# Routing two chunks at once in a convolution and mixture-of-experts kernel, and a written order for the tile loads

## The chip, the cores and the metric

The kernel runs on one core of one Trainium2 chip. The metric is the time of one execution in device microseconds (us). The core's engines are TensorE (PE; PEld is its weight load), VectorE (DVE), ScalarE (ACT), GpSimd (POOL) and SyncE (SP, which here only issues transfers). The 16 DMA engines carry what SP and POOL issue.

## The reference

A causal convolution of width 7, whose weights differ per position and head (softmax over the seven taps), gives x of 28672 rows by 192. Each row then goes to one of eight experts, the one with the highest logit, and the expert's two-layer network is scaled by the gate's probability:

```
w = softmax(weight_gen, axis=-1)                      # (8, 3584, 8, 7)
x[s, h, g] = sum_k w[s, h, k] * x_pad[s + k, h, g]     # 28672 x 192
logits = x @ w_gate;  e = argmax(logits);  gate = softmax(logits)[e]
y = gate * (relu(x @ w1[e]) @ w2[e])                   # w1 192x1024, w2 1024x192
```

## The kernel before

The rows are worked in 28 chunks of 1024 (128 partitions by J = 8 columns). For a chunk c, DVE makes the convolution (`taps`: seven multiplications and six additions of 1536 elements per partition, written as L386 and L410; the first five chunks get help from PE and POOL), ACT and DVE split the result into two f16 parts in the payload buffer `pl` (`high`, `low`, three buffers), PE transposes it (L506), and `finish(c)` routes it: 24 small matmuls for the logits (`logits`), a row of short DVE operations that find the expert (`route1`), nine narrow matmuls that count ranks (`ranks`), the gate factor (`gate`), the place of every row in its expert's queue (`places`), and `send(c)`, in which POOL scatters the chunk's eight columns of rows to the `queue` in DRAM by eight indirect transfers (helper line L589). At the end `choose(c)` runs `select` (seven short DVE operations, L603 to L618), which takes as many full tiles of 384 rows from the eight queues as the plan says. `make_plan` fixes that number before the run: it keeps up to HOLD = 6 tiles' worth of rows back, so that every tile taken is of one expert. Chunks 1 to 4 give tiles of 256 rows, chunks 5 to 26 two or three tiles of 384 (one for chunk 5), chunk 27 the rest: tiles of 384, 256 and 128 and padded short ones.

`experts()` works the tiles n = 0, 1, 2, ... in order. `fetch(n)` issues on SP: a load of the tile's first row number from `rows` (L809, waits for `select`), the transposed rows `xt` (L825, waits until the scatters of all chunks up to the tile's chunk have landed), the expert's weights `wt` (L827, 1.8 MB, three buffers, so it waits until PE has ended the second layer of tile n - 3) and `meta` (L830, the rows' gate factor and destination). PE makes the first layer (L890, five matmuls for each of eight groups), ACT the relu `hh` (L910), DVE the low part `hl` (L913), PE the second layer (L787), ACT the scaled output `o` (L791, six buffers), and POOL scatters `o` to the output (L589). The first-layer results stand in four PSUM buffers `ph`, the second-layer results in four `y` slots. For some tiles PE and ACT make the low part in place of DVE (L899, L903, L905).

DVE's order is written out by the program: a planner holds a clock of DVE (`clock[0]`) and of PE (`clock[1]`), takes the low parts when they are due, then routing steps, then the convolution, and adds a cost for each. The other engines' order comes from the scheduler of the framework, which goes by its own estimate and by priorities; routing steps stand at high priority. Each engine works its instructions in order.

Of the kernel before, what the change touches and what calls it, by code (L numbers as in the profile page):

```python
# [28 lines left out]
ROW = 392  # L29
# [3 lines left out]
J = 8  # L33
# [3 lines left out]
SUBS = 6  # L37
LATE_SUBS = 18
STEP = 0.2
# [80 lines left out]
def conv_moe_kernel(ctx: ExitStack, tc: tile.TileContext, x, wgen, w_gate, w1, w2, out):  # L120
# [42 lines left out]
    nc.vector.tensor_scalar(negi, identf, -1.0, None, op0=ALU.mult)  # L163
    revE = const.tile([P, J, E], F32, name="revE")
    nc.gpsimd.iota(revE, pattern=[[0, J], [-1, E]], base=E, channel_multiplier=0,
                   allow_small_or_imprecise_dtypes=True)
# [5 lines left out]
    nc.vector.tensor_scalar(room, base0[0:1, :], -1.0, float(TOP), op0=ALU.mult, op1=ALU.add)  # L172
    oh_t = []
    for i in range(2):
        t = const.tile([P, J + 1, E], F16, name=f"oh{i}")
        nc.gpsimd.memset(t, 0.0)
        oh_t.append(t)
    eg_t = []
    for i in range(2):
        t = const.tile([P, J, E + 1], F32, name=f"eg{i}")  # L180
        nc.gpsimd.memset(t[:, :, E:], 1e-9)
        eg_t.append(t)
# [270 lines left out]
    def scale(c):  # L453
# [57 lines left out]

    def logits(c):
        k = ch[c]
        k.pm = ps_m.tile([P, 512], F32, name="pm")
        k.lp = k.pm[:, 0:J * 2 * E].rearrange("p (j t e) -> p j t e", j=J, t=2)
        for j in range(J):
            for n in range(3):
                nc.tensor.matmul(k.lp[:, j], k.xg[:, 3 * j + n, :], gw[:, n], start=(n == 0), stop=(n == 2))  # L518
                clock[1] += GATE

    def route1(c):
        k = ch[c]
        k.lg = rt.tile([P, J, E], F32, name="lg")
        k.eg = eg_t[c % 2]
        nc.vector.tensor_reduce(k.lg, k.lp.rearrange("p j t e -> p j e t"), axis=AX.X, op=ALU.add)
        yield STEP
        lm = rt.tile([P, J], F32, name="lm")
        nc.vector.tensor_reduce(lm, k.lg, axis=AX.X, op=ALU.max)
        yield STEP
        nc.vector.tensor_tensor(k.lg, k.lg, lm.unsqueeze(2).to_broadcast([P, J, E]), op=ALU.subtract)  # L530
        nc.scalar.activation(k.eg[:, :, 0:E], k.lg, AF.Exp, scale=k.lsc)
        yield STEP
        pri = rt.tile([P, J, E], F32, name="pri")
        nc.vector.scalar_tensor_tensor(pri, k.lg, 0.0, revE, op0=ALU.is_ge, op1=ALU.mult)
        yield STEP
        pmx = rt.tile([P, J], F32, name="pmx")
        nc.vector.tensor_reduce(pmx, pri, axis=AX.X, op=ALU.max)
        yield STEP
        k.oh = oh_t[c % 2]
        nc.vector.tensor_tensor(k.oh[:, 0:J, :], pri, pmx.unsqueeze(2).to_broadcast([P, J, E]), op=ALU.is_equal)  # L540

    def ranks(c):
        k = ch[c]
        k.rp = k.pm[:, 256:256 + (J + 1) * E].rearrange("p (j e) -> p j e", j=J + 1)
        nc.tensor.matmul(k.rp, tri, k.oh, start=True, stop=False)
        for j in range(J):
            nc.tensor.matmul(k.rp[:, j + 1:, :], ones_h, k.oh[:, j:j + 1, :].to_broadcast([P, J - j, E]),
                             start=False, stop=(j == J - 1))
        clock[1] += 0.3

    def gate(c):
        k = ch[c]
        se = rt.tile([P, J], F32, name="se")
        nc.vector.tensor_reduce(se, k.eg, axis=AX.X, op=ALU.add)
        yield STEP
        nc.vector.tensor_tensor(se, se, k.rsx.to_broadcast([P, J]), op=ALU.mult)
        yield STEP
        nc.vector.reciprocal(k.pl.bitcast(F32)[:, :, D], se)
        yield STEP

    def places(c):
        k = ch[c]
        rk = rt.tile([P, J, E], F32, name="rk")
        bs = base[-1]
        nc.vector.tensor_tensor(rk, k.rp[:, 0:J, :], bs.unsqueeze(1).to_broadcast([P, J, E]), op=ALU.add)
        nb = rt.tile([P, E], F32, name="nb", bufs=3)
        nc.vector.tensor_tensor(nb, k.rp[:, J, :], bs, op=ALU.add)
        base.append(nb)
        yield STEP
        nc.vector.tensor_tensor(rk, rk, k.oh[:, 0:J, :], op=ALU.mult)  # L570
        yield STEP
        k.pos = rt.tile([P, J], I32, name="pos")
        with nc.allow_low_precision("queue positions are whole numbers below 2**24"):
            nc.vector.tensor_reduce(k.pos, rk, axis=AX.X, op=ALU.add)
        yield STEP

    def send(c):
        k = ch[c]
        for j in range(J):
            st = scatter(queue, k.pos[:, j:j + 1], k.pl[:, j, 0:ROW // 2], "q")  # L580
            tc.add_to_no_dep_group(f"s{c}", st.ins)
            writers[c].append(st.ins.name)
        sent[0] = c
# [84 lines left out]
    rest = []  # L668
    first_ = []
    sent = [0]  # L670
    writers = [[] for _ in range(NCH)]
# [122 lines left out]
    def fetch(n):  # L794
# [44 lines left out]
    def experts():  # L839
# [25 lines left out]
        while True:  # L865
# [13 lines left out]
            for t in range(groups):  # L879
# [253 lines left out]
```

## Time and profile before

| what | value |
|---|---|
| median of 3 runs | 1186.94 us (1186.53 to 1188.32) |
| the profiled execution | 1185.47 us |
| its span in the profile | 1183.8 us |
| PE busy | 1123.8 us, 95% of the span |
| DVE busy | 1034.9 us, 87% |
| POOL busy | 696.3 us, 59% |
| ACT busy | 647.1 us, 55% |

The span runs from the first to the last instruction in the profile; 1.7 us of the profiled execution lie around it. Busy shares are averages over stages: the first fifth of the span is the start, with the weights' preparation and the first chunks; then convolution and experts run side by side until the last chunk is routed near 1012 us; from there on only tiles are left.

### The profile page before, as it was taken

What the parts mean: (1) busy time and instruction counts of PE and PEld (TensorE: products, weight loads), DVE (VectorE), ACT (ScalarE), POOL (GpSimd) and SP (SyncE); (2) the same over time, 40 slices, a digit from 0 to 9 for tenths busy, and PEclk for the clock granted to TensorE, in tenths of its full rate; (3) what the DMA queues carried; (4) which work ended last, traced back from release to release, by engine and by line L of the source; (5) the groups of instructions that cost most, each with busy time, mean ns of one, the idle gap of its engine ahead of it and who ended that gap; (6) DMA issues with size and microseconds to landing.
All of it is one profiled execution on the core that took longest, in us unless ns stands there. A gap on an engine that the chain in (4) does not pass through costs nothing. (4 is left out here: it accounts for less than half of the span.)

```text
span 1183.8 us, 29289 instructions
## 1 busy us (share of the span) xinstructions
PE 1123.8 (95%) x11327; PEld 913.1 (77%) x11327; DVE 1034.9 (87%) x1771; ACT 647.1 (55%) x1348; POOL 696.3 (59%) x633
## 2 busy tenths in 40 slices
PE   5689799999999999999999999999999999999996
PEld 3455489998778878787788888787777777778996
DVE  7999999999999999999999999999999997833231
ACT  3555477777556555545554555656465556443342
POOL 7998647766654654664566566447555675721222
PEclk9999899999999999999999999999999999999999
DMA  9989899999889787888898788777687666799993
GB/s 280 378 299 335 248 335 308 307 307 307 254 219 279 239 257 229 258 240 232 221 290 237 209 276 260 234 209 236 235 242 245 196 151 223 235 330 353 351 344 136
DMA packets 182847, 311.44 MB, mean 263 GB/s; under 512 B 131243, under 2 KB 154785, under 8 KB 167470
## 3 DMA queue, kind: packets, MB, share of 16 engines
q1 hardware_dynamic: 160702, 264.17, 73.3%
q0 software_dynamic: 22000, 45.33, 12.0%
q8 instruction: 91, 1.49, 0.5%
q14 instruction: 54, 0.44, 0.1%
HBM read 226.97 MB, written 60.45 MB: 243 GB/s over the span
## 5 line engine op out<-in xcount | busy, mean ns | idle before, releaser
L890 PE MATMUL ph<-xt,wt 128*128 128x384 f16 (+6 forms) x3680 | 571.2, 296 | 9.5 <-DVE hl L913 5.5
L787 PE MATMUL yo<-wt,hh 128*128 128x192 f16 (+1 forms) x3648 | 489.8, 246 | 2.9 <-ACT o L791 2.9
L589 POOL DMA_INDIRECT out_dram<-o,meta x228 | 281.1, 1233 | 323.5 <-ACT o L791 254.5
L787 PE MATMUL yo<-wt,hl 128*128 128x192 f16 (+1 forms) x1824 | 438.3, 246 | 0.0
L890 PEld LDWEIGHTS <-wt 128*128 128x128 f16 x3680 | 317.7, 98 | 124.3 <-issue 6.4
L910 ACT ACTIVATE hh<-ph 128x384 f16<-128x384 f32 (+2 forms) x485 | 238.5, 495 | 292.9 <-PE ph L890 272.1
L913 DVE SCALAR_TENSOR_TENSOR hl<-ph,hh 128x384 f16<-128x384 f32 (+2 forms) x485 | 260.4, 552 | 110.7 <-ACT hh L910 110.2
L787 PEld LDWEIGHTS <-hh 128*128 128x128 f16 (+1 forms) x3648 | 330.2, 98 | 32.9 <-issue 3.7
L589 POOL DMA_INDIRECT queue<-pl,pos x224 | 289.7, 1293 | 98.6 <-issue 72.9
L386 DVE TENSOR_TENSOR tv<-x_sb,wp 128x1536 f32<-128x1536 f32 (+1 forms) x173 | 286.2, 1656 | 1.7 <-PE ph L395 1.4
L410 DVE TENSOR_TENSOR acc<-acc,tv 128x1536 f32<-128x1536 f32 x138 | 239.6, 1736 | 0.0
L787 PEld LDWEIGHTS <-hl 128*128 128x128 f16 (+1 forms) x1824 | 178.7, 98 | 18.5 <-ACT hl L905 0.2
L791 ACT ACTIVATE o<-yo,fac 128x192 f32<-128x192 f32 (+1 forms) x228 | 90.5, 418 | 89.5 <-PE yo L787 85.1
L508 ACT ACTIVATE xg<-ph 128x1024 f16<-128x1024 f16 x84 | 81.6, 1022 | 38.2 <-PE ph L506 38.0
L395 PE MATMUL ph<-tv,identf 128*128 128x384 f32 x210 | 82.6, 539 | 17.8 <-DVE tv L386 17.1
L395 PEld LDWEIGHTS ph<-tv,identf 128*128 128x128 f32 x210 | 41.4, 209 | 45.2 <-DVE tv L386 19.0
L899 ACT ACTIVATE hh<-ph 128x512 f16<-128x512 f32 (+1 forms) x88 | 48.9, 562 | 22.1 <-PE ph L890 16.0
L447 ACT ACTIVATE junk<-x_sb 128x768 bf16<-128x768 f32 (+2 forms) x56 | 48.0, 857 | 16.1 <-DVE ssq L456 6.0
L905 ACT ACTIVATE hl<-ph 128x512 f16<-128x512 f32 (+1 forms) x88 | 47.7, 559 | 10.6 <-PE ph L903 10.2
L506 PE MATMUL ph<-idh,pl 128*128 128x128 f16 x672 | 52.3, 219 | 0.4 <-DVE pl L500 0.3
L486 ACT ACTIVATE pl<-acc 128x768 f16<-128x768 f32 (+1 forms) x51 | 39.0, 805 | 15.3 <-DVE acc L410 9.2
L506 PEld LDWEIGHTS <-pl 128*128 128x128 f16 x672 | 42.7, 98 | 5.9 <-ACT pl L491 2.6
(133 smaller groups left out, 768.9 us busy)
## 6 DMA issues: line engine op xcount, KB each, us to landing
wt<-wq SPq DMA_DIRECT2D x92, 1796.0 KB
x_sb<-in_x_dram SPq DMA_DIRECT2D x27, 1344.0 KB
w_sb<-in_weight_gen_dram SPq DMA_DIRECT2D x28, 224.0 KB
wq<-ws SPq DMA_DIRECT2D x8, 772.0 KB
f<-in_moe_w_dram SPq DMA_DIRECT2D x8, 768.0 KB
f<-in_moe_w_dram SPq DMA_DIRECT2D x8, 512.0 KB
wq<-ws SPq DMA_DIRECT2D x8, 512.0 KB
wq<-ws SPq DMA_DIRECT2D x32, 128.0 KB
```

The costliest lines, as they stand in the source:

```text
L386: eng.tensor_tensor(out, xs, ws, op=ALU.mult)
L395: nc.tensor.matmul(ap[:, 0:m], identf, tf[:, 2 * i * D:2 * i * D + m], start=(n == 0), stop=(n == KW - 1))
L410: eng.tensor_tensor(ac, ac, t, op=ALU.add)
L506: nc.tensor.transpose(pt[:, m, :], p16[:, j, n * P:(n + 1) * P], idh)
L508: nc.scalar.activation(k.xg[:, i:i + 8, :], pt, AF.Copy)
L589: st = nc.gpsimd.indirect_dma_start(out=dst, out_offset=bass.IndirectOffsetOnAxis(ap=idx, axis=0), in_=src, in_offset=None, **kw)
L787: nc.tensor.matmul(y, hx[:, f, sl], w2v[:, f, t, :], start=(f == 0 and k == 0), stop=(f == NF - 1 and k == 2))
L791: nc.scalar.activation(o[0:m, :], y, AF.Copy, scale=fac[0:m, s:s + 1])
L890: nc.tensor.matmul(ph[:, g], wt[:, wc + f * P:wc + (f + 1) * P], xt[:, xc, 0:T], start=(k == 0 and g == 0), stop=(k == 4), skip_group_chec ...
L899: nc.scalar.activation(hv, ph, AF.Relu, scale=SHRINK)
L910: nc.scalar.activation(hv, ph, AF.Relu)
L913: nc.vector.scalar_tensor_tensor(lv, ph, 0.0, hv, op0=ALU.max, op1=ALU.subtract)
```

## The change

Four pairs of chunks, (6, 7), (8, 9), (10, 11) and (12, 13), are routed together. The first chunk of a pair ends after its logits matmuls, which go to the first half of a PSUM tile that both share; the second chunk's routing then works on both at once, with operands twice as wide, sends the rows of both (16 indirect transfers in a row) and chooses the tiles of both in one `select`. `make_plan` gives the first of a pair no tile and the second those of both (5, 6, 5 and 5 tiles); the number and sizes of all tiles stay as they were. New buffers: a third one-hot tile `oh` and exponent tile `eg` of double width, each with a memset on POOL at the start; `revE` is a row that is broadcast. The reciprocal in `gate` and the exponential on ACT stay one for each chunk.

On SP, an order is written down: for tiles of chunks 18 to 26 the weights are issued before the transposed rows, which follow them; for tiles of chunks 5 to 15 the rows follow `meta` of the tile before. The last line of the diff writes a condition in another way, with the same tiles on either side of it.

```diff
+PAIRED = (6, 8, 10, 12)
+LATE_FROM = 18
@@ t_main
-        return [T_MAIN]
+        return [] if c in PAIRED else [T_MAIN]
...
@@ scale
-        k.rsx = rt.tile([P, 1], F32, name="rsx", bufs=4)
+        if c - 1 in PAIRED:
+            k.rsx = ch[c - 1].rsx2[:, 1:2]
+        else:
+            k.rsx2 = rt.tile([P, 2], F32, name="rsx", bufs=4)
+            k.rsx = k.rsx2[:, 0:1]
@@ logits
+        at = 0
+        if c - 1 in PAIRED:
+            k.pm, at = ch[c - 1].pm, J
+        else:
+            k.pm = ps_m.tile([P, 512], F32, name="pm")
+        k.n = at + J
+        k.lp = k.pm[:, 0:k.n * 2 * E].rearrange("p (j t e) -> p j t e", j=k.n, t=2)
...
+    def members(c):
+        return [ch[c - 1], ch[c]] if ch[c].n > J else [ch[c]]
@@ route1
+        n = k.n
+        sh = [P, n, E]
...
+        nc.vector.tensor_tensor(lg, lg, lm.unsqueeze(2).to_broadcast(sh), op=ALU.subtract)
+        for i, m in enumerate(members(c)):
+            nc.scalar.activation(k.eg[:, i * J:i * J + J, 0:E], lg[:, i * J:i * J + J], AF.Exp, scale=m.lsc)
...
@@ ranks
+        k.rp = k.pm[:, 256:256 + (n + 1) * E].rearrange("p (j e) -> p j e", j=n + 1)
         nc.tensor.matmul(k.rp, tri, k.oh, start=True, stop=False)
+        for j in range(n):
+            nc.tensor.matmul(k.rp[:, j + 1:, :], ones_h, k.oh[:, j:j + 1, :].to_broadcast([P, n - j, E]),
+                             start=False, stop=(j == n - 1))
@@ gate
+        for i, m in enumerate(ms):
+            nc.vector.reciprocal(m.pl.bitcast(F32)[:, :, D], se[:, i * J:i * J + J])
+            yield STEP
...
@@ send
+        for i, k in enumerate(members(c)):
+            for j in range(J):
+                st = scatter(queue, ch[c].pos[:, i * J + j:i * J + j + 1], k.pl[:, j, 0:ROW // 2], "q")
...
@@ finish
         logits(c)
+        if c in PAIRED:
+            return
         yield from route1(c)
@@ fetch
-        rows_of(nc.sync.dma_start_transpose(xt[:, :, 0:T], q16[ds(r, T), 0:2 * D]))
         wt = pw.tile([P, WROW], F16, name="wt")
-        nc.sync.dma_start(wt, wq[ds(e * P, P), :])
+        behind = LATE_FROM <= c < NCH - 1
+        if behind:
+            before_[:] = [nc.sync.dma_start(wt, wq[ds(e * P, P), :]).ins.name]
+        x_ = nc.sync.dma_start_transpose(xt[:, :, 0:T], q16[ds(r, T), 0:2 * D])
+        rows_of(x_)
+        if behind or PAIRED[0] - 2 < c < PAIRED[-1] + 4:
+            tc.add_manual_dep(x_.ins, before_[0], mybir.DependencyInfo(
+                mybir.DependencyClass.NoSync, mybir.DependencyReason.DATA), reason="order on SP")
+        if not behind:
+            nc.sync.dma_start(wt, wq[ds(e * P, P), :])
...
         rows_of(m)
+        before_[:] = [m.ins.name]
@@ experts
-                if ((n % 8 == 1 and todo[n][3] >= LATE_SUBS) or todo[n][3] < SUBS) and todo[n][3] < NCH - 3:
+                if todo[n][3] < SUBS or (n % 8 == 1 and LATE_SUBS <= todo[n][3] < NCH - 3):
```

## Rows read from the trace of the kernel before

**Rows 1.** The page, busy time, share of the span and instructions of each engine (first row), and the span in 40 equal slices, busy share in tenths, of PE and DVE.

```profile
PE 1123.8 (95%) x11327; PEld 913.1 (77%) x11327; DVE 1034.9 (87%) x1771; ACT 647.1 (55%) x1348; POOL 696.3 (59%) x633
...
PE   5689799999999999999999999999999999999996
...
DVE  7999999999999999999999999999999997833231
```

**Rows 2.** Busy time by stretch (us from the span's start). Columns: stretch and length, then busy us (and instructions) of PE, PEld, DVE, ACT and POOL, granted clock, share of the DMA engines, GB/s.

```profile
250.00:700.00 450.00, 449.72 (x4531) 365.44 (x4530) 443.03 (x737) 257.36 (x549) 270.38 (x219) 1.00 0.87 255
700.00:800.00 100.00, 99.93 (x982) 79.61 (x981) 97.92 (x165) 57.18 (x128) 54.14 (x47) 1.00 0.77 231
800.00:900.00 100.00, 96.78 (x968) 76.95 (x965) 97.67 (x159) 58.07 (x122) 65.64 (x50) 1.00 0.74 234
900.00:1000.00 100.00, 97.01 (x970) 76.99 (x971) 94.95 (x161) 54.11 (x115) 56.83 (x46) 1.00 0.70 204
1000.00:1100.00 100.00, 98.66 (x907) 79.53 (x905) 49.20 (x135) 39.94 (x92) 39.95 (x42) 1.00 0.95 302
1100.00:1184.00 84.00, 72.23 (x1135) 71.41 (x1132) 21.42 (x33) 31.54 (x72) 21.23 (x23) 0.97 0.81 271
```

**Rows 3.** The waits of PE from 700 us to the end: who waited for whom, us in total, times, longest.

```profile
PE ph L890 <- DVE hl L913: 5.5, 9, 1.3
PE yo L787 <- ACT o L791: 2.3, 5, 0.7
...
PE ph L890 <- DMA xt<-queue: 1.4, 1, 1.4
```

**Rows 4.** The timeline of PE in the middle of the span, in two stretches: start, length, line, operation, operands, how many in the piece. The last row is the first group of tile 31, the first tile of chunk 12.

```profile
500.36 0.98 PE L890 MATMUL ph<-xt,wt 128*128 128x384 f16 x5
501.17 0.25 PE L787 MATMUL yo<-wt,hl 128*128 128x192 f16 x1
501.25 0.25 PE L787 MATMUL yo<-wt,hh 128*128 128x192 f16 x1
...
508.57 0.35 PE L547 MATMUL pm<-oh,ones_h 128*128 128x64 f16 x8
508.79 0.81 PE L890 MATMUL ph<-xt,wt 128*128 128x384 f16 x4
...
509.76 0.98 PE L890 MATMUL ph<-xt,wt 128*128 128x384 f16 x5
```

**Rows 5.** DVE's instructions by line and form, 270 to 560 us: operands, shapes, how many; busy us and mean ns of one; idle time before.

```profile
L498 DVE TENSOR_TENSOR pl<-acc,pl 128x1024 f16<-128x1024 f32 x7 | 8.4, 1204 | 0.0
...
L500 DVE TENSOR_TENSOR pl<-acc,pl 128x512 f16<-128x512 f32 x7 | 4.7, 669 | 0.0
...
L603 DVE TENSOR_TENSOR free<-room,step 1x72 f32<-1x72 f32 x8 | 2.0, 250 | 0.0
L525 DVE TENSOR_REDUCE lg<-pm 128x64 f32<-128x128 f32 x7 | 2.0, 285 | 1.5 <-PE pm L518 1.5
...
L558 DVE RECIPROCAL pl<-se 128x8 f32<-128x8 f32 x8 | 1.5, 190 | 0.0
...
L567 DVE TENSOR_TENSOR nb<-pm,nb 128x8 f32<-128x8 f32 x8 | 1.2, 151 | 0.0
```

**Rows 6.** The timeline of DVE around a `select` step: start, length.

```profile
849.41 0.15 DVE L615 TENSOR_SCALAR rows<-top 1x8 int32<-1x8 f32 x1
849.48 0.28 DVE L616 SCALAR_TENSOR_TENSOR key<-key,top,free 1x72 f32<-1x72 f32 x1
849.68 1.20 DVE L498 TENSOR_TENSOR pl<-acc,pl 128x1024 f16<-128x1024 f32 x1
```

**Rows 7.** The timeline of SP in two stretches: start and length of the issue of `xt` (L825) and `wt` (L827).

```profile
858.87 1.32 SPq L825 DMA_TRANSPOSE xt<-queue  x1
860.51 0.36 SPq L827 DMA_DIRECT2D wt<-wq  x1
...
884.92 0.33 SPq L827 DMA_DIRECT2D wt<-wq  x1
896.44 1.34 SPq L825 DMA_TRANSPOSE xt<-queue  x1
...
972.68 0.36 SPq L827 DMA_DIRECT2D wt<-wq  x1
```

**Rows 8.** The timeline of PE at the start of tile 60 (900.35, the tile whose `wt` and `xt` are issued at 884.92 and 896.44) and of tile 66 (982.60, `wt` issued at 972.68).

```profile
900.35 0.81 PE L890 MATMUL ph<-xt,wt 128*128 128x384 f16 x4 [1.42 <-DMA xt<-queue]
...
982.60 0.65 PE L890 MATMUL ph<-xt,wt 128*128 128x384 f16 x3
```

**Rows 9.** The timeline of POOL: the first and the last of the eight scatters of chunk 9 (316.08, 326.31) and of chunk 13 (477.46, 490.25); in square brackets the idle time before.

```profile
316.08 1.72 POOL L589 DMA_INDIRECT queue<-pl,pos  x1 [4.08 <-DVE pos L574]
...
326.31 0.96 POOL L589 DMA_INDIRECT queue<-pl,pos  x1 [0.30 <-issue]
...
477.46 2.15 POOL L589 DMA_INDIRECT queue<-pl,pos  x1 [3.84 <-issue]
...
490.25 0.96 POOL L589 DMA_INDIRECT queue<-pl,pos  x1 [0.30 <-issue]
```

**Rows 10.** The outputs `o` on ACT, 270 to 560 us: how many; ns of one, min/median/max; first and last start.

```profile
L791 ACT ACTIVATE o<-yo,fac x65: 400/415/441, 272.0 to 556.9; 128x192 f32<-128x192 f32 x65
```

**Rows 11.** The waits of SP, 690 to 1010 us.

```profile
SPq L809 <- DVE key L616: 80.7, 9, 14.7
```

More of the change, by code (lines that the diff above doesn't have):

```diff
@@ L163, in conv_moe_kernel @@
     nc.vector.tensor_scalar(negi, identf, -1.0, None, op0=ALU.mult)
-    revE = const.tile([P, J, E], F32, name="revE")
-    nc.gpsimd.iota(revE, pattern=[[0, J], [-1, E]], base=E, channel_multiplier=0,
+    revE = const.tile([P, E], F32, name="revE")
+    nc.gpsimd.iota(revE, pattern=[[-1, E]], base=E, channel_multiplier=0,
                    allow_small_or_imprecise_dtypes=True)
@@ L172, in conv_moe_kernel @@
     nc.vector.tensor_scalar(room, base0[0:1, :], -1.0, float(TOP), op0=ALU.mult, op1=ALU.add)
-    oh_t = []
-    for i in range(2):
-        t = const.tile([P, J + 1, E], F16, name=f"oh{i}")
+    oh_t, eg_t = [], []
+    for i in range(3):
+        t = const.tile([P, (1 + i // 2) * J + 1, E], F16, name=f"oh{i}")
         nc.gpsimd.memset(t, 0.0)
         oh_t.append(t)
-    eg_t = []
-    for i in range(2):
-        t = const.tile([P, J, E + 1], F32, name=f"eg{i}")
+        t = const.tile([P, (1 + i // 2) * J, E + 1], F32, name=f"eg{i}")
         nc.gpsimd.memset(t[:, :, E:], 1e-9)
@@ L513, in logits @@
         k = ch[c]
-        k.pm = ps_m.tile([P, 512], F32, name="pm")
-        k.lp = k.pm[:, 0:J * 2 * E].rearrange("p (j t e) -> p j t e", j=J, t=2)
+        at = 0
[5 more added lines that the diff above has]
+        k.lp = k.pm[:, 0:k.n * 2 * E].rearrange("p (j t e) -> p j t e", j=k.n, t=2)
         for j in range(J):
             for n in range(3):
-                nc.tensor.matmul(k.lp[:, j], k.xg[:, 3 * j + n, :], gw[:, n], start=(n == 0), stop=(n == 2))
+                nc.tensor.matmul(k.lp[:, at + j], k.xg[:, 3 * j + n, :], gw[:, n], start=(n == 0), stop=(n == 2))
@@ L519, in logits @@
                 clock[1] += GATE
+    def members(c):
+        return [ch[c - 1], ch[c]] if ch[c].n > J else [ch[c]]
     def route1(c):
         k = ch[c]
-        k.lg = rt.tile([P, J, E], F32, name="lg")
-        k.eg = eg_t[c % 2]
-        nc.vector.tensor_reduce(k.lg, k.lp.rearrange("p j t e -> p j e t"), axis=AX.X, op=ALU.add)
+        n = k.n
+        sh = [P, n, E]
+        pd = dict(padded_shape=[P, 2 * J, E])
+        i = 2 if n > J else c % 2
+        lg = rt.tile(sh, F32, name="lg", **pd)
+        k.eg, k.oh = eg_t[i], oh_t[i]
+        nc.vector.tensor_reduce(lg, k.lp.rearrange("p j t e -> p j e t"), axis=AX.X, op=ALU.add)
@@ L526, in route1 @@
         yield STEP
[L527 to L528 removed]
+        lm = rt.tile([P, n], F32, name="lm", padded_shape=[P, 2 * J])
+        nc.vector.tensor_reduce(lm, lg, axis=AX.X, op=ALU.max)
         yield STEP
[L530 to L531 removed]
+        nc.vector.tensor_tensor(lg, lg, lm.unsqueeze(2).to_broadcast(sh), op=ALU.subtract)
@@ L545, in ranks @@
         nc.tensor.matmul(k.rp, tri, k.oh, start=True, stop=False)
[L546 to L549, printed above, removed]
+        for j in range(n):
+            nc.tensor.matmul(k.rp[:, j + 1:, :], ones_h, k.oh[:, j:j + 1, :].to_broadcast([P, n - j, E]),
+                             start=False, stop=(j == n - 1))
+        clock[1] += 0.3 * n / J
@@ L551, in gate @@
     def gate(c):
         k = ch[c]
-        se = rt.tile([P, J], F32, name="se")
+        n = k.n
+        se = rt.tile([P, n], F32, name="se", padded_shape=[P, 2 * J])
         nc.vector.tensor_reduce(se, k.eg, axis=AX.X, op=ALU.add)
         yield STEP
-        nc.vector.tensor_tensor(se, se, k.rsx.to_broadcast([P, J]), op=ALU.mult)
+        ms = members(c)
+        r = ms[0].rsx2[:, 0:n // J]
+        sj = se.rearrange("p (c j) -> p c j", j=J)
+        nc.vector.tensor_tensor(sj, sj, r.unsqueeze(2).to_broadcast([P, n // J, J]), op=ALU.mult)
@@ L557, in gate @@
         yield STEP
-        nc.vector.reciprocal(k.pl.bitcast(F32)[:, :, D], se)
-        yield STEP
+        for i, m in enumerate(ms):
+            nc.vector.reciprocal(m.pl.bitcast(F32)[:, :, D], se[:, i * J:i * J + J])
+            yield STEP
     def places(c):
         k = ch[c]
-        rk = rt.tile([P, J, E], F32, name="rk")
+        n = k.n
+        sh = [P, n, E]
+        rk = rt.tile(sh, F32, name="rk", padded_shape=[P, 2 * J, E])
         bs = base[-1]
-        nc.vector.tensor_tensor(rk, k.rp[:, 0:J, :], bs.unsqueeze(1).to_broadcast([P, J, E]), op=ALU.add)
+        nc.vector.tensor_tensor(rk, k.rp[:, 0:n, :], bs.unsqueeze(1).to_broadcast(sh), op=ALU.add)
@@ L566, in places @@
         nb = rt.tile([P, E], F32, name="nb", bufs=3)
-        nc.vector.tensor_tensor(nb, k.rp[:, J, :], bs, op=ALU.add)
+        nc.vector.tensor_tensor(nb, k.rp[:, n, :], bs, op=ALU.add)
         base.append(nb)
         yield STEP
-        nc.vector.tensor_tensor(rk, rk, k.oh[:, 0:J, :], op=ALU.mult)
+        nc.vector.tensor_tensor(rk, rk, k.oh[:, 0:n, :], op=ALU.mult)
         yield STEP
-        k.pos = rt.tile([P, J], I32, name="pos")
+        k.pos = rt.tile([P, n], I32, name="pos", padded_shape=[P, 2 * J])
@@ L577, in send @@
     def send(c):
[L578 to L582, printed above, removed]
+        for i, k in enumerate(members(c)):
+            for j in range(J):
+                st = scatter(queue, ch[c].pos[:, i * J + j:i * J + j + 1], k.pl[:, j, 0:ROW // 2], "q")
+                tc.add_to_no_dep_group(f"s{c}", st.ins)
+                writers[c].append(st.ins.name)
         sent[0] = c
@@ L669, in conv_moe_kernel @@
     first_ = []
+    before_ = []
     sent = [0]
```

11 lines of the change are left out of this document (5 added, 6 removed).

## The prediction

> **What bounds the kernel now.** I read the page's busy shares first. PE leads with 95% of the span, DVE has 87%, and the slices show both near full from the fifth slice on, DVE until about the 34th [rows 1]. Two engines near full means that the share of one says little, so I went on to the stretches. From 250 to 700 us PE is busy 449.7 of 450 us; DVE is busy 443.0 [rows 2]. From 700 on the two come apart: PE is idle for 0.1, 3.2, 3.0 and 1.3 us in the four hundreds up to 1100, 7.6 us together. Soon after 1000 us DVE has only the tiles' low parts left (its busy time halves in that hundred, PE's doesn't), and PE works off what was kept back. So PE sets the end, and only two things can move it: work taken from PE, or idle time of PE taken away.
>
> A busy PE need not be a PE at its pace, so I looked at its timeline. Five first-layer matmuls of 384 columns take 0.81 us from start to start, 0.162 us each, and a second-layer one 0.08 us [rows 4]. That is 384 and 192 columns at 2.4 GHz to within a few per cent, with the clock granted in full [rows 2]. The middle of the span is therefore PE work with no air in it, about 40 x 0.162 + 72 x 0.082 = 12.4 us for a tile.
>
> Which waits make the idle time after 700? The waits of PE name DVE's low part (5.5 us, nine times), the output on ACT (2.3 us) and once the rows of a tile (1.4 us) [rows 3]. None is long. They belong together: SP waits 80.7 us in this stretch for `select` to have run [rows 11], so tiles are fetched as soon as they are chosen. In 250 to 700 us tiles were chosen faster than needed or from a reserve; here the reserve is used up. Tile 60 shows it. Its weights go out at 884.92, its rows at 896.44 us, and PE starts at 900.35 after a wait of 1.42 us for those rows [rows 7, 8]. DVE at 95 to 98% is late with chunks, PE runs dry for moments, and DVE in its turn stands for 2 to 5% because PE is late with the tiles whose low parts come next in its order [rows 2].
>
> **The change part by part.** *PE.* The logits matmuls are the same. Ranks are 17 matmuls for a pair in place of 18. Eight narrow ones take 0.22 us from start to start [rows 4]. The pair's are up to twice as wide: 136 x 8 + 136 = 1224 columns, 0.51 us at the columns' pace that the 384-column matmuls show, against about 0.5 us for two single sets. Zero. The tiles are the same in number and size, so PE's work doesn't change at all.
>
> *DVE.* A chunk's routing is 13 short operations, from 285 ns (L525) to 151 ns (L567), 2.68 us together; `select` is seven of about 0.23 us (250 ns for L603), 1.60 us [rows 5]. A pair pays 13 operations that are wider, one more reciprocal, and one `select` instead of two. The width costs 1.05 ns for an element, from 1204 and 669 ns for 1024 and 512 elements [rows 5]. Eight operations get 64 elements more (8 x 67 ns), the first reduction 128 (0.13 us), the sum of exponentials 72 (0.08 us), the rest nothing that counts, the second reciprocal costs 0.19 us (L558): 0.94 us more. By durations a pair then takes 2.68 + 0.94 + 1.60 = 5.22 us instead of 2 x 4.28 = 8.56: 3.3 us less. Durations overlap, though. An operation of 0.15 us is followed by the next start after 0.07 us, one of 0.28 after 0.20 [rows 6], so about 0.08 us of each doesn't count, and 40 operations become 21. That takes 19 x 0.08 = 1.5 us off the saving: 1.8 us. Bounds for four pairs: 7.2 us by starts, 13.3 us by durations. I take 7.2, since DVE in this stretch is full and works by starts.
>
> This saving is made before about 500 us (chunk 13's scatters end at 491.21 [rows 9]), where PE doesn't wait for DVE. There it is worth nothing directly; it goes into lead. The planner fills DVE's free time with the next convolution, so every later chunk is chosen at least 7.2 us earlier. Where PE ran dry after 700 us, each wait shrinks by as much of the lead as is not yet spent. The waits add up to 7.6 us of idle time [rows 2], the lead is 7.2 us plus the 2 to 5% that DVE no longer stands. So nearly all 7.6 us go; and as each wait also hides the drain of a matmul (0.25 us shown for one that follows the next after 0.08 [rows 4]), up to 0.17 us more for each of the 15 waits in [rows 3], 2.5 us, could come on top. I take 7.6, and 0 and 10 as ends.
>
> *Choosing later.* Tiles of a pair's first chunk are chosen with the second. The reserve covers this where it is largest. The tightest place is tile 31, the first of chunks 12 and 13, which PE starts at 509.76 us [rows 4]. Chunk 13's eight scatters run from 477.46 to 491.21 us [rows 9]. Sixteen at that pace end at 505.0 us with no lead at all, and rows need at most 3.9 us from issue to use (896.44 to 900.35) [rows 7, 8]: 508.9, just before. With the lead gained by then it is some 5 us better. Cost zero, at worst 2 or 3 us once.
>
> *POOL.* No operation more per chunk, but 16 scatters in a row with the outputs `o` queued behind them. Eight take 11.2 us (chunk 9) to 13.75 us (chunk 13), and POOL stood 3.8 to 4.1 us before the first, as the scatters stand in its order already [rows 9]. Sixteen: 22.4 + 3.8 = 26.2 to 27.5 + 4.1 = 31.6 us. An output comes every 4.45 us (64 steps in 284.9 us) [rows 10], and six buffers hold 26.7 us. So 0 to 4.9 us for which ACT stands with the relus behind it. PE goes on in that time in the four `ph` buffers; a group is 0.81 us of first layer and nine second-layer matmuls, 1.55 us, four are 6.2 us. Covered; I take zero, and 4 x 4.9 = 19.6 us if the cover is gone.
>
> *SP.* The order for chunks 5 to 15 only keeps a tile's blocked rows from standing ahead of the preceding tile's weights: zero. From chunk 18 on weights go first. For tile 60 that was so already [rows 7]; for tile 58 the rows went 1.6 us ahead, so its weights gain 1.6 us. What could be late is the rows. Tile 66 started 9.9 us after its weights' issue without a wait [rows 7, 8], so weights take at most 9.9 us, and rows behind them at most 9.9 + 3.9 = 13.8 us if the two are carried one after the other. A tile lasts 12.4 us, so the bound doesn't exclude a loss of 1.4 us for each of the 24 tiles (47 to 70). But 1.8 MB at the 204 to 302 GB/s that these stretches moved with gaps is 6 to 9 us, so I take zero, up to 34 us. The Trainium skill, "DMA: Bandwidth & Descriptors", section "Queues, rings and completion order", says that an engine takes the descriptors of one ring in their order; by it the rows start behind all of the weights, and the sum stays as it is while weights take under 8.5 us. No row here shows the order of the packets themselves.
>
> The memsets at the start stand on POOL while the first chunk is being loaded: zero.
>
> **The rivals.** *A, forecast:* the waits after 700 us go. 1185.5 - 7.6 = 1177.9 us for the profiled execution, which stands 1.5 us under the median; against the median 1186.9 - 7.6 = 1179.3 us. With the ends: 1177 to 1184.
>
> *B, no change:* the waits for the low part (5.5 of 9.2 us in [rows 3]) come from DVE's order, which ties each low part behind a convolution step, not from missing tiles. Then a lead doesn't remove them. Against it: there are none from 250 to 700 us with DVE just as full [rows 2]. 1186.9 us, plus or minus 2.
>
> *C, slower by POOL:* the 16 scatters outlast the six output buffers. It decides from 26.7 us of blocked POOL; at 31.6 us and without cover 19.6 us are lost, less the 7.6 gained: 1199 us. For it: chunk 13's block; against it: the cover above.
>
> *D, more:* if PE had room in the middle, DVE's whole saving would show, up to 13.3 us: 1173.6 us. Against it stands PE's pace. The Trainium skill, "Perfetto Trace Analysis", section "Identifying the Most-Contended Engine", says that busy time of matmuls tells little and that the weight loads' busy share is the better measure; that share is 81% in the middle [rows 2], which would leave PE a fifth and make DVE the bound. The starts in [rows 4] disagree, and they decide.
>
> *E, slower by SP:* rows behind weights come late from chunk 18 on. It decides where weights take more than 12.4 - 3.9 = 8.5 us; from 0.3 us a tile it eats the gain, at 1.4 us for 24 tiles it gives 1186.9 - 7.6 + 34 = 1213 us. Against it: tile 60's weights were issued 11.5 us before its rows and hid wholly.
>
> **How the numbers follow.** Chances: A 0.68, B 0.12, C 0.08, D 0.05, E 0.07. This kernel's measurement tells 0.2%, 2.4 us, from no change. Faster is A and D, 0.73; within 0.2% is B and the mild half of E, 0.15; slower is C and the rest of E, 0.12. The predicted time is A's, 1179.3 us. The range goes from the lower half of D's reach (1175) to B's middle (1187).
>
> **What would show it.** PE's idle time from 700 to 1100 us under 2 us, no wait for rows or low parts there; DVE's busy time between 1000 and 1100 us lower by some 5 us, as the last chunk is routed earlier; POOL's blocks of 16 scatters near 25 us with no idle time of PE behind them; routing lines on DVE with 24 instead of 28 instructions and 270 to 280 ns for the wide ones. Wrong it would be if PE shows idle time between 250 and 560 us (C, or late rows), or waits for `xt` after 720 us (E), or if the waits for low parts stay with tiles at hand (B).

## The result: 0.85% slower, and the profile after

The changed kernel takes 1196.67 us (1195.26 to 1199.76) against 1186.99 us for the kernel before in the same comparison: ratio 1.0085, interval 1.0070 to 1.0100. The time lies above the forecast of 1179.3 us and above its whole range (1175 to 1187 us). The profiled execution took 1198.93 us, with a span of 1196.7 us.

The page of the changed kernel, which answers to [rows 1]: busy shares, then three of the lines in 40 slices.

```profile
PE 1129.2 (94%) x11323; PEld 915.8 (77%) x11323; DVE 1034.7 (86%) x1695; ACT 649.0 (54%) x1348; POOL 696.4 (58%) x635
...
PE   5689799997999999999999999999999999989997
...
DVE  7999999898799999999999999999999997723231
...
PEclk9899899998899999999999999999999999989999
```

DVE has 76 instructions fewer, 19 for each pair. PE does the same work (four matmuls fewer, one for each pair), yet its slices show a 7 from 269 to 299 us and an 8 from 1047 to 1077 us. The windows of the changed kernel, with columns as in [rows 2], put sizes to both:

```profile
250.00:300.00 50.00, 40.20 (x469) 37.56 (x466) 45.67 (x51) 32.85 (x62) 36.12 (x29) 0.93 0.70 236
300.00:350.00 50.00, 48.85 (x465) 37.49 (x466) 42.72 (x67) 29.56 (x65) 25.92 (x21) 0.93 0.93 274
700.00:800.00 100.00, 99.88 (x984) 78.86 (x982) 98.12 (x162) 57.37 (x128) 56.90 (x46) 1.00 0.79 236
800.00:900.00 100.00, 99.94 (x1006) 80.21 (x1005) 98.01 (x159) 58.98 (x125) 62.11 (x53) 1.00 0.82 255
900.00:1000.00 100.00, 99.38 (x967) 78.83 (x966) 98.96 (x165) 55.00 (x118) 51.94 (x41) 1.00 0.71 196
1000.00:1100.00 100.00, 94.89 (x872) 74.13 (x871) 49.31 (x140) 41.02 (x91) 43.24 (x45) 0.97 0.91 282
```

What was forecast for 700 to 1000 us happened: PE is idle for 0.8 us in place of 6.3 [rows 2]. But a stretch that had no idle time before, 250 to 300 us, has lost 9.8 us, and 1000 to 1100 us has lost 5.1. The waits of PE for its first layer over the whole span name two transfers:

```profile
PE ph L928 <- DMA wt<-wq: 13.7, 3, 10.5
PE ph L928 <- DMA xt<-queue: 5.0, 1, 5.0
PE ph L928 <- DVE hl L951: 1.3, 3, 0.7
```

The wait of 10.5 us is for weights, and the DMA engines were nearly free just ahead of it. Here are the windows around it:

```profile
280.00:290.00 10.00, 10.00 (x117) 9.58 (x116) 9.10 (x9) 5.84 (x12) 8.17 (x7) 1.00 0.19 63
290.00:301.00 11.00, 0.65 (x12) 0.47 (x9) 6.57 (x4) 3.94 (x6) 7.16 (x8) 0.63 0.90 245
301.00:306.00 5.00, 4.85 (x32) 2.83 (x33) 0.00 (x0) 1.49 (x4) 0.98 (x1) 0.50 1.07 379
```

A DMA share of 0.19 ahead of the wait means that no large load was under way. SP's timeline shows why; the rows are the weights of tile 13, its `meta`, and the rows and weights of tile 14:

```profile
263.75 0.33 SPq L864 DMA_DIRECT2D wt<-wq  x1
290.74 0.39 SPq L867 DMA_DIRECT2D meta<-queue  x1
291.32 1.43 SPq L857 DMA_TRANSPOSE xt<-queue  x1
293.06 0.35 SPq L864 DMA_DIRECT2D wt<-wq  x1
```

SP issued nothing from 264.1 to 290.7 us, and then a transfer of 2 KB. Its longest wait, 22.6 of these 27 us, is for that transfer's buffer. Here are SP's waits of this kind over the whole span; the first row is of the kernel before (a row that I had not read), the second of the changed kernel:

```profile
SPq L830 <- DMA out_dram<-o,meta: 37.4, 17, 8.4
```

```profile
SPq L867 <- DMA out_dram<-o,meta: 124.7, 22, 22.6
```

`meta` holds the destination rows of a tile. The output scatter on POOL reads them as its index, so a `meta` buffer is free only when the tile's outputs have gone. There are four buffers: tile 13's waits for the outputs of tile 9. POOL's timeline shows where those stood, from the last output ahead of the pair's 16 scatters to the first behind them:

```profile
254.78 0.98 POOL L614 DMA_INDIRECT out_dram<-o,meta  x1 [1.94 <-DVE acc L410]
258.49 0.96 POOL L614 DMA_INDIRECT queue<-pl,pos  x1 [2.73 <-issue]
...
285.29 0.96 POOL L614 DMA_INDIRECT queue<-pl,pos  x1 [0.30 <-issue]
286.56 0.99 POOL L614 DMA_INDIRECT out_dram<-o,meta  x1 [0.30 <-issue]
```

The granted clock fell to one half 2.2 us into the wait, at 292.9 us, and stayed there until 306.5 us, so PE started the next tile at half its pace. The same five matmuls that take 0.81 us in [rows 4] take 1.6 us from start to start:

```profile
301.15 1.78 PE L928 MATMUL ph<-xt,wt 128*128 128x384 f16 x5 [10.50 <-DMA wt<-wq]
302.73 0.37 PE L815 MATMUL yo<-wt,hl 128*128 128x192 f16 x1
```

A sum over PE's matmuls, each one's time from start to start less the median of its kind, puts the difference in its places: from 200 to 350 us the changed kernel loses 19.2 us where the one before lost 1.7; from 800 to 1000 us it loses 2.4 instead of 9.3; from 1000 to 1100 us 7.8 instead of 1.9. That is +17.5, -6.9 and +5.9 us, 16.5 together, against 12.9 us between the spans; the first 150 us, 3.5 us shorter in this execution, make most of the rest.

Not all of the 17.5 us lie at 290 us. The wait there and the half clock behind it make 13.2. The other 4.4 us are an earlier wait, before the first pair is routed, at 204.8 us, again with half the clock behind it (from 207.5 to 210.9 us):

```profile
207.72 2.32 PE L928 MATMUL ph<-xt,wt 128*128 128x256 f16 x10 [2.94 <-DMA wt<-wq]
```

This is the start of tile 6. Until 192.7 us SP had stood 7.4 us for tile 5's `meta`, behind an ordinary block of eight scatters (0.9 us at most in the kernel before at that place), and tile 6's weights went out at 196.1 us, where the version with seven `meta` (below) sends them at 193.1 us, with tile 5 starting within 0.3 us of the same time. It is the same mechanism without the longer block.

The vanished idle time of 700 to 1000 us needs a second look too: a PE that has just lost some 17 us may give DVE lead by that alone. The version with seven `meta` (below) hasn't lost them, and its windows show 0.8 us of idle time as well:

```profile
700.00:800.00 100.00, 99.88 (x980) 79.72 (x979) 99.08 (x169) 55.93 (x122) 57.17 (x48) 1.00 0.83 247
800.00:900.00 100.00, 99.77 (x1003) 79.60 (x1002) 98.04 (x159) 59.14 (x127) 56.65 (x48) 1.00 0.76 234
900.00:1000.00 100.00, 99.56 (x1003) 79.61 (x1001) 91.36 (x163) 55.80 (x116) 56.76 (x47) 1.00 0.72 201
```

### The profile page after: what moved, and what is told of

It is laid out like the page before. It is cut to its first block, busy times and chain, and to the rows that moved or that the text cites. A ratio compares the mean times of both kernels' runs of the same rounds, so it can differ in the third digit from the quotient of the medians.

```text
span 1196.7 us, 29197 instructions
## 1 busy us (share of the span) xinstructions
PE 1129.2 (94%) x11323; PEld 915.8 (77%) x11323; DVE 1034.7 (86%) x1695; ACT 649.0 (54%) x1348; POOL 696.4 (58%) x635
## 4 chain that ended last, share of the span: by engine, by line
PE 59%; DVE 12%; issue 12%; DMA 9%; POOL 5%; SPq 1%; ACT 1%; POOLq 0%; DVEq 0%; ACTq 0%
PE ph L928 29%; PE yo L815 25%; DMA f<-in_moe_w_dram 4%; DVE tv L386 3%; POOL out_dram L614 3%; PE ph L510 2%; DVE acc L410 2%; DVE hl L951 2%; DMA wt<-wq 2%; POOL queue L614 1%; PE pm L528 1%; PE ph L941 1%; DMA queue<-padrow,padi 1%; DMA wq<-ws 1%; DMA xt<-queue 1%
## 5 line engine op out<-in xcount | busy, mean ns | idle before, releaser
L928 PE MATMUL ph<-xt,wt 128*128 128x384 f16 (+6 forms) x3680 | 575.2, 299 | 20.1 <-DMA wt<-wq 13.7
L614 POOL DMA_INDIRECT out_dram<-o,meta x228 | 277.7, 1218 | 336.5 <-ACT o L819 280.9
L614 POOL DMA_INDIRECT queue<-pl,pos x224 | 293.1, 1308 | 101.8 <-issue 80.7
L351 POOL TENSOR_TENSOR w_sb<-w_sb,mx 128x448 f32<-128x448 f32 x27 | 29.3, 1084 | 31.9 <-DVE mx L350 24.4
```

The source lines that it names most:

```text
L614: st = nc.gpsimd.indirect_dma_start(out=dst, out_offset=bass.IndirectOffsetOnAxis(ap=idx, axis=0), in_=src, in_offset=None, **kw)
L928: nc.tensor.matmul(ph[:, g], wt[:, wc + f * P:wc + (f + 1) * P], xt[:, xc, 0:T], start=(k == 0 and g == 0), stop=(k == 4), skip_group_chec ...
```

## The experiments

The theory after the first look, M: the block of 16 scatters delays outputs, these hold `meta`, `meta` holds SP, and SP holds the next weights. Rivals: O, the written order on SP is to blame; C, the six `o` (the prediction's own rival); R, the rows of a pair are chosen and sent late; and for the rest, T, the stream of weights at the end takes back what is gained earlier.

Eight kernels were run beside a kernel before at 1186.1 to 1186.5 us; the others fell on chips on which the kernel before itself took 1285 to 1303 us, with PE waiting again and again for nothing that the profile names, and of those only ratios and waits at the place in question are used.

**Seven `meta`.** In the changed kernel:

```diff
-        meta = px.tile([P, 4, 2], F32, name="meta", bufs=AHEAD + 1 if ring else 4)
+        meta = px.tile([P, 4, 2], F32, name="meta", bufs=AHEAD + 1 if ring else 7)
```

> The changed kernel with seven buffers for meta alone, once more. Theory M: no long wait near 290 us, the one near 1045 us stays; ratio to the kernel before 0.994 to 0.999. Rival R: the wait at 290 us stays, ratio 1.005 or more.

Measured: 1186.32 us (1183.63 to 1189.51), ratio 1.0002 [0.9987, 1.0017]. One buffer count gives back 10 us; the gain over the kernel before that M also forecast (0.994 to 0.999) is not there. Of this kernel the waits of PE for transfers and SP's wait for `meta`, whole span, then SP's timeline at the place:

```profile
PE ph L928 <- DMA xt<-queue: 4.9, 1, 4.9
PE ph L928 <- DMA wt<-wq: 2.7, 5, 1.3
```

```profile
SPq L867 <- DMA out_dram<-o,meta: 4.5, 5, 2.9
```

```profile
259.39 0.33 SPq L864 DMA_DIRECT2D wt<-wq  x1
259.99 0.38 SPq L867 DMA_DIRECT2D meta<-queue  x1
264.77 4.82 SPq L857 DMA_TRANSPOSE xt<-queue  x1
276.48 0.36 SPq L864 DMA_DIRECT2D wt<-wq  x1
```

Tile 13's `meta` follows its weights at once, tile 14's weights go 16.6 us earlier, and the granted clock in 250 to 350 us is 1.00. M holds for this place and R falls. PE's waits for the output on ACT stay at 0.8 us in the whole middle, with and without the edit, and the wait at 205 us is gone too. The wait of 4.9 us for rows near 1030 us stays, so it has another cause.

The same edit in the kernel before and in the changed kernel, on one of the other chips:

> The kernel before with seven buffers for meta. If M holds only through the longer block, the 37.4 us for which SP waits for outputs in the kernel before are hidden, and the time stays at 1185 to 1188 us. If meta limits the kernel before too, part of the 7.6 us of PE's idle time between 700 and 1100 us goes: 1179 to 1184 us.

> The changed kernel with seven buffers for meta in place of four, nothing else. Theory M (the block of 16 scatters holds back the outputs of tile 9, so the fourth-next meta finds no free buffer, SP stands on it 22.6 us with the loads of tile 14 behind it): SP's wait of meta for outputs falls from 124.7 to under 30 us, PE's wait of 10.5 us at 290 us and the half clock after it (13.7 us at 0.5) are gone, and the time falls by about 13 us to 1183 to 1185 us. Rival R (tile 14 and 15 are late because the rows of a pair are chosen and sent late): the wait at 290 us stays and the time stays at 1194 to 1198 us.

Measured: ratios 0.9977 [0.9952, 1.0003] and 1.0124 [1.0091, 1.0156]. More `meta` do nothing that can be told for the kernel before. The second ratio differs from the 1.0002 above; on this chip PE's longest waits name no cause, and what the pairs do to them is not settled.

**Pairs alone, and the written order alone.** The first has SP's order as before, with four `meta`; the second has no pairs:

```diff
-PAIRED = (6, 8, 10, 12)
+PAIRED = ()
...
-        if behind or PAIRED[0] - 2 < c < PAIRED[-1] + 4:
+        if behind or 4 < c < 16:
```

> The pairs without the written order, once more, with four buffers for meta. Theory M: the wait for weights near 290 us is there with or without the order; ratio 1.003 to 1.010. Rival O (the written order puts tile 14's loads behind the blocked meta): no such wait, ratio 0.990 to 0.998.

> The written order on SP alone, chunks routed one by one. Theory M: blocks are of 8 scatters, so no long wait for meta; PE's idle time from 700 us on as in the kernel before or a little less: 1184 to 1188 us. Rival O: rows stand behind blocked metas here too, and the time is 1189 us or more. Rival E of the prediction (rows behind weights come late from chunk 18 on): waits for xt after 720 us, 1190 us or more.

Measured: pairs alone 1194.74 us, ratio 1.0084 [1.0067, 1.0100] (1.0176 [1.0127, 1.0225] on one of the other chips); the order alone, there, 0.9984 [0.9959, 1.0009]. So the order is not what costs, and O falls. But pairs alone is no copy of the changed kernel. Its SP timeline, with tile 13's weights, the rows of tiles 14 and 15, tile 13's `meta` and tile 14's weights:

```profile
261.30 0.33 SPq L855 DMA_DIRECT2D wt<-wq  x1
266.68 20.99 SPq L853 DMA_TRANSPOSE xt<-queue  x2
288.40 0.40 SPq L858 DMA_DIRECT2D meta<-queue  x1
289.12 0.33 SPq L855 DMA_DIRECT2D wt<-wq  x1
```

Here tile 15's rows, which wait until the pair's scatters have landed, stand ahead of tile 14's weights, and PE waits 8.5 us. The written order takes the rows out of the way, and then `meta` is found standing there for the same 16 scatters. Order and seven `meta` together free the place. Seven `meta` without the order was not run; that the rows alone would still hold SP there is argued from the 14.9 us for which SP waits for the scatters in this run.

**The block cut in two.** The second chunk's eight scatters were to stand 14 us later in the order (`yield 14.0` between them in `send`).

> The changed kernel with four buffers for meta, but the sixteen scatters of a pair sent as two blocks of eight, some 14 us apart in DVE's order, so that outputs come between. Theory M (the length of the block holds the outputs): the wait at 290 us is gone or under 3 us, SP's wait of meta for outputs well under 124.7 us, ratio 0.994 to 1.000. If not the block but the pair's late choice is to blame, the wait stays or grows by the 14 us: ratio 1.008 or more.

Measured: 1194.22 us, ratio 1.0088 [1.0060, 1.0117]. Inconclusive on the block's length: POOL ran all 16 as one block again (254.28 to 280.85 us), since the order is DVE's and POOL's own stayed. SP waited 19.4 us for `meta`, and PE 4.5 us for weights behind it.

**Without the first pair.** `PAIRED = (8, 10, 12)`, four `meta`, the written order kept for the same chunks:

> The changed kernel without its first pair: chunks 6 and 7 are routed one by one, (8, 9), (10, 11) and (12, 13) in pairs; four buffers for meta, the written order as it is. Theory M: a block of 16 scatters hurts only where tiles of 256 rows follow each other at 8 to 10 us and no further tile's data is at hand, which is at the first pair; the later blocks hold meta too, but hidden behind tiles of 12.4 us. So no wait of PE over 2 us between 250 and 560 us, ratio to the kernel before 0.995 to 1.001. If every block of 16 costs PE time, a wait shows at one of the other three pairs and the ratio is 1.003 or more.

Measured: 1185.51 us (1182.17 to 1190.08), ratio 1.0001 [0.9990, 1.0012]. With four `meta` the three later pairs cost nothing, so the changed kernel's 10 us hang on the first pair (the wait at 205 us is absent here too). SP still waits for `meta` up to 9.8 us there, but the tiles at the later pairs have 384 rows instead of 256 and last longer.

**The second wait.** Near 1040 us SP's timeline of the changed kernel shows rows, weights, rows: tile 71's rows, the first of chunk 27, wait 5.8 us for the queues' padding and stand ahead of the weights and then the rows of tile 70, which the new order (L856) puts one behind the other. For tile 71 no order was written. The rows are tile 71's `xt`, tile 70's `wt`, and the `xt` of tile 70 and the next in one row:

```profile
1037.39 1.33 SPq L857 DMA_TRANSPOSE xt<-queue  x1
1039.03 0.36 SPq L856 DMA_DIRECT2D wt<-wq  x1
1039.52 8.62 SPq L857 DMA_TRANSPOSE xt<-queue  x2
```

Seven `meta` and one more condition:

```diff
-        if behind or PAIRED[0] - 2 < c < PAIRED[-1] + 4:
+        if behind or PAIRED[0] - 2 < c < PAIRED[-1] + 4 or (late and n == lates[1]):
```

> The changed kernel with seven buffers for meta, and the written order also for the first tile of chunk 27, so that its rows (which wait for the padding of the queues) can't be issued ahead of the loads of tile 70. Theory M, and the second wait of the changed kernel (5.2 us near 1045 us) being that inversion on SP: both waits gone, PE's idle time from 250 us to 1100 us under 3 us, no half clock between 145 us and the end; the ratio to the kernel before 0.988 to 0.994. Rival R (rows of a pair sent late): the wait at 290 us stays, ratio over 1.002.

Measured: 1185.72 us (1181.67 to 1189.33), ratio 1.0000 [0.9986, 1.0015]. This version, seven `meta` and the condition for tile 71, is called the mended change from here on. The wait near 1030 us is gone, but the time is that of seven `meta` alone, not the 0.988 to 0.994 expected. In the profiled execution most of the 4.9 us turn up again near the end, as a wait of 3.28 us at tile 91, the last one ahead of `last_tiles`:

```profile
1161.76 0.29 PE L928 MATMUL ph<-xt,wt 128*128 128x32 f16 x4 [3.28 <-SPq L1146]
```

Tile 78 starts 7.9 us earlier than in the kernel before (1108.7 against 1116.6 us), tile 91 only 5.4 us (1161.8 against 1167.2), half a microsecond after its weights' last packet at 1161.3 us. The small tiles 78 to 85 take PE 4.2 us each; from one tile's last weight packet to the next pass 5.2 to 7.7 us, about 6 on average. (The profile names a line behind the loop, `SPq L1146`, as the releaser; that it is the weights is read from their last packet.)

**Less weight at the end (T).** Tiles 78 to 91 load 5136 of 7184 weight columns, and their first layer reads other columns in place of those left out, so its result is another; the work is the same. Once on the version just above, once on the kernel before:

```diff
-            nc.sync.dma_start(wt, wq[ds(e * P, P), :])
+            wc = O_H1 if late and lates[1] + AHEAD <= n < len(todo) else WROW
+            nc.sync.dma_start(wt[:, 0:wc], wq[ds(e * P, P), 0:wc])
...
```

> Seven buffers for meta and the written order for the first tile of chunk 27, and from the eighth tile of the last chunk on (tiles 78 to 91) only the first 5136 of 7184 columns of the weights are loaded, 28% less; the matmuls of these tiles that would read the rest read the first columns instead, in the same number and shape, so part of the first layer's result is replaced for those rows. Theory T (the last tiles are held by the stream of weights, 6.3 us for each at 4.2 us of PE work, which takes back the lead of the late stretch): PE's wait of 3.4 us at tile 91 goes, the time falls by 2 to 5 us against the same kernel with whole weights, ratio to the kernel before 0.995 to 0.998. If the lead is lost elsewhere, the ratio stays at 0.999 to 1.001.

> The kernel before with the same shorter weights for tiles 78 to 91 (part of the first layer's result of those rows is replaced). Theory T: PE's wait there was 1.46 us, so 0 to 2 us are gained, ratio 0.998 to 1.000, less than in the kernel with pairs. If shorter weights gain 3 us or more here too, the tail holds both kernels alike and is not where the lead went.

Measured: 1178.87 us, ratio 0.9944 [0.9930, 0.9958], and 1182.76 us, ratio 0.9977 [0.9967, 0.9988]. Shorter transfers are worth 6.9 us (1185.72 to 1178.87) with the mended change and 3.7 us (1186.48 to 1182.76) without it, by the ratios 6.6 and 2.7 us, more than expected in both. The mended change is worth 3.9 us where the end is short (some 2 us either way by the intervals) and none where it isn't.

T is not settled by this. The sign against it, 3 us or more in the kernel before too, is met by the medians and not by the ratio, and its own share is a difference of 3 to 4 us between two gains that are uncertain by 1 to 2.5 us each. The profiled executions show less: from 1100 us on the kernel before loses 4.0 us against the medians of its matmuls and the mended change 4.9, and with shorter weights both lose 1.1 to 1.2, so the end takes back 1 us there. And about 1 us of each gain is not the weights': the matmuls of tiles 74 and 75 came in another order, without a wait of 1.1 and 0.8 us for a low part.

**Both mends and three pairs.** Seven `meta`, the condition for tile 71, no first pair:

> As the kernel with three pairs, with seven buffers for meta and the written order for the first tile of chunk 27: everything that the runs so far point to, put together. Both long waits gone; if the last tiles are held by the stream of their weights, the gain of the late stretch ends there and the ratio is 0.996 to 0.999; if nothing holds it, 7.6 us are gained and the ratio is 0.992 to 0.995.

Measured: 1196.0 us (1192.25 to 1199.77), ratio 1.0082 [1.0063, 1.0101]. Not expected: two edits that cost nothing with four pairs cost 10 us together with three. Its trace has C's mechanism, behind the 16 scatters of chunks 10 and 11. First POOL, then ACT, whose output waits for a free `o`, then PE:

```profile
393.22 2.50 POOL L614 DMA_INDIRECT queue<-pl,pos  x1 [0.30 <-issue]
...
419.50 0.99 POOL L614 DMA_INDIRECT out_dram<-o,meta  x1 [0.30 <-ACT o L819]
```

```profile
424.05 0.42 ACT L819 ACTIVATE o<-yo,fac 128x192 f32<-128x192 f32 x1 [3.17 <-DMA out_dram<-o,meta]
429.69 0.42 ACT L819 ACTIVATE o<-yo,fac 128x192 f32<-128x192 f32 x1 [5.21 <-DMA out_dram<-o,meta]
```

```profile
424.52 0.33 PE L815 MATMUL yo<-wt,hh 128*128 128x192 f16 x2 [1.99 <-ACT o L819]
...
430.16 0.48 PE L815 MATMUL yo<-wt,hh 128*128 128x192 f16 x2 [2.48 <-ACT o L819]
```

With the half clock behind it this costs 8 us against the run with four `meta`, where the same block held ACT for 1.9 us at most. In that run `meta` kept SP quiet while the outputs drained (its rows go out at 420.62 us); with seven, weights and rows go out at 410.80 and 412.62 us, and the outputs at 419.50 and 420.79 us free their `o` late. That the traffic slows them is argued, not shown.

**More `o`, and one more `meta`.** Twelve `o` for six, in the last kernel, in the version with four pairs, and in the changed kernel as it was (room was made by cutting the late ring's `xt` to 256 rows); and the changed kernel with five `meta`:

```diff
-        ffo = ctx.enter_context(tc.tile_pool(name="ffo", bufs=6, reuse_waits="tile"))
+        ffo = ctx.enter_context(tc.tile_pool(name="ffo", bufs=12, reuse_waits="tile"))
```

> Three pairs, seven meta, the first late tile's rows behind the loads ahead of it (the version that took 1196.0 us), now with 12 output tiles o in place of 6; to make room, the late ring's xt tiles are cut to 256 rows and a late tile of 384 rows takes an xt of the ordinary three. If the 16 scatters of the pair 10 and 11 held TensorE there through the six o tiles (TensorE waited 2.0 and 2.5 us at 422 to 430 us, and ran at half the clock behind that), those two waits and the low clock behind them are gone and the time comes to 1184 to 1188 us. If something else made that version slow, it stays at 1193 to 1198 us.

> The changed kernel with seven meta, the first late tile's rows behind the loads ahead of it (1185.7 us so far) and 12 output tiles o, with the same cut of the late xt tiles. If the o tiles cost nothing once the four pairs are there, and the last weights' stream sets the end, it stays at 1185 to 1187 us; if the spread of that version from execution to execution (1181.7 to 1189.3 us) comes from the six o tiles, it comes to 1181 to 1184 us with less spread.

> The changed kernel with 12 output tiles o in place of 6 (and the cut of the late xt tiles), meta as it was with four. The buffer that the prediction named as the one that a block of 16 scatters could exhaust was o. If o is what is short, the wait of 10.5 us near 290 us goes and the time falls to 1186 us; if meta is, the wait stays and the time stays at 1194 to 1198 us.

> The changed kernel with five meta in place of four. In the changed kernel tile 13's meta waits for the outputs of tile 9, which stand behind the block of 16 scatters; with five it waits for those of tile 8. If tile 8's outputs were all scattered before the block (the last output ahead of it went at 254.8 us), one meta more is enough, and the time comes to 1185 to 1188 us as with seven; the next tile then waits in tile 13's place, for tile 9, and if it is due before 290 us, a part of the 10 us stays (1188 to 1194 us). If meta is not the cause, it stays at 1195 to 1198 us.

All fell on the other chips, the first two in two runs each. Ratios: 1.0054 [1.0021, 1.0087] and 1.0144 [1.0102, 1.0187] for the first; 1.0097 [1.0054, 1.0140] and 1.0102 [1.0066, 1.0137] for the second; 1.0165 [1.0082, 1.0247] and 1.0102 [1.0067, 1.0138] for the others. Against each other these times decide nothing. The wait on SP does for the third: twelve `o`, 200 to 400 us:

```profile
SPq L868 <- DMA out_dram<-o,meta: 32.4, 5, 20.6
```

Its longest part is there hardly diminished (22.6 us in the changed kernel), and PE waits 5.5 us for weights behind it: `o` is not what was short at the first pair (C falls there). With five `meta` SP's wait falls to 8.6 us in the same stretch, and PE has no wait for weights there. Whether more `o` mend the version with three pairs stays open.

## Why the prediction was wrong

**Where it held.** PE sets the end, and its work is unchanged. DVE pays 19 operations less for a pair; the routing has 24 instructions where there were 28, the wide ones at 277 to 287 ns against 270 to 280 forecast. DVE's busy time from 1000 to 1100 us, forecast to fall by some 5 us, falls from 49.2 to 45.9 us with seven `meta` (in the changed kernel itself, 13 us late, it doesn't). The idle time of 700 to 1000 us was a starved reserve and went with the lead, in the version with seven `meta` too (A's mechanism, B falls). Rows behind weights from chunk 18 on were not late but for tile 70 at the edge (E falls in its place). D needs room in PE that nothing showed: with the waits gone PE in the changed kernel is busy 99.94 of 100 us from 800 to 900 us at the same times from start to start. The Trainium skill, "Perfetto Trace Analysis", section "Identifying the Most-Contended Engine", would read a fifth of PE as free from the weight loads' 80% there; the trace disagrees.

**The step that failed: "POOL", with "Choosing later", both put at zero.** The block was sized rightly: from the end of the last output ahead of it to the first output behind it 30.8 us pass, forecast 26.2 to 31.6. Wrong was whom it holds. I asked only which buffers the outputs fill, the six `o`, found PE covered by four `ph`, and put zero. I did not ask which buffers the output scatters read. `meta` is the other operand in the row's own name, `out_dram<-o,meta`; it has four buffers, and it waits not on ACT but on SP, ahead of the next tile's rows and weights. The warning stood in the profile before: SP's 17 waits for `meta`, 37.4 us, up to 8.4 us with blocks of eight. From there: tile 13's `meta` went at 263.8 us before and could have gone as late as 276.5, when tile 14's weights went; a block twice as long put it at 290.74, 14 us too late. PE's wait of 10.5 us is most of that. Nor is the cover by four `ph` sure: where `o` did run short, in the run with three pairs and both mends, ACT stood 3.2 and 5.2 us and PE still 2.0 and 2.5.

**The tightest place.** I took the last pair (tile 31), where a chunk's worth of lead is spent, and not the first, where tiles have 256 rows, follow each other after 7 to 10 us, and the same buffers cover less time. The run without the first pair says that with four `meta` the whole loss hung on it.

**The price of a stall.** I counted idle time only. The wait cost its 10.5 us and then, with the clock low until 306.5 us, another 2.7 us: 5.4 us of work from 301.15 us on at half the pace.

**SP.** "Zero" for the written order forgot its edge: the first tile behind the ordered stretch keeps no order, and its blocked rows went ahead of the ordered pair. That is 5.0 us of waiting in the profiled execution; taking it away changed the median by nothing that can be told.

**The gain.** With `meta` mended the forecast time of 1179.3 us still didn't come: 1185.7 us. The step "nearly all 7.6 us go" treated the end of the kernel as something that only shifts. The end can hold PE by itself: the same view of the kernel before from which [rows 3] come has one row more, `PE ph L890 <- SPq L1108: 1.5, 1, 1.5`, and that is the wait of tile 91. With the last weights shortened 3.9 us of the 7.6 show. How much of that the stream of whole weights takes back is open, and the other 3.7 us are not accounted for in full. About 2 us of them lie in 200 to 350 us, where the mended change loses 3.7 us to the kernel before's 1.7. What the typical execution loses no trace shows: the profiled one of the mended change was its fastest, 1181.67 us, 4 us under its median and 3.8 under the profiled execution of the kernel before.

## What to carry to other kernels

Before you lengthen a block on an in-order queue, list every buffer that the work behind the block releases, its inputs and indices as well as its outputs, and for each the queue on which the next user waits and what stands behind that user. A wait that costs nothing before (37 us of a quiet SP) is the place to look at first. And price a gain at the end of the kernel too: if the last stretch has another bound, work that arrives earlier may only wait there.

## What the runs showed of the hardware

PE's granted clock fell to 0.50, that is 1.2 GHz, 2.2 us into the 10.5 us without work, and stayed there for 13.7 us, from 292.9 us on; from 301 to 306 us PE was busy 97% of the time, and 384-column matmuls took 0.32 us in place of 0.16. Shorter waits were followed by the same: 2.94 us at 204.8 us in the changed kernel (0.50 from 207.5 to 210.9 us), 2.13 us at 264.7 us in the run with the block cut in two (0.50 from 266.6 us for 3.4 us), and the waits of 2.0 and 2.5 us in the run with three pairs and both mends (0.73 in 430 to 440 us). In the kernel before no such stretch lies between 142 us and the last tiles.

A GpSimd indirect transfer of 128 rows takes 0.96 us and the next starts 0.30 us later, when nothing else is in the way; more than a quarter of the changed kernel's 224 take 1.5 us or longer, up to 3.0, so its four blocks of 16 took 23.6 to 27.8 us where 16 of the short ones would take 20.
